# Batch 0 of an attention-and-MLP kernel: scores before transposes, a second load queue, an earlier normalise at the seam

## The chip, the cores and the metric

The kernel runs on one core of one Trainium2 chip. The metric is the device time of one execution in microseconds (us), as the median of several executions. "Span" is the part that the profile covers, about 1.8 us less than the time. Each run also lists the mean clock granted to TensorE (PE), where 1.000 means that no half-speed stretch is on record. The clock's record begins 4.6 to 7.1 us into the span, so the first warm-up matmuls, which start 0.43 us apart, twice the 0.216 us seen later at a granted clock of 1.00, are not in it.

## The reference

For 8 batches, 12 heads, 448 positions and a head size of 64, softmax attention with one added to the denominator; the result, as 3584 rows of 768, goes through a two-layer MLP with a squared ReLU.

```
scores = q @ k.T / 8
e      = exp(scores - max)
attn   = e / (sum(e) + exp(-max) + 1e-09)
x      = (attn @ v), heads side by side      # 3584 x 768
out    = (relu(x @ w_in) ** 2) @ w_out       # 768 -> 2048 -> 768
```

## The kernel before

Work goes by *units*. A unit is one pair of heads of one batch. Batch 0 is cut in two (192 and 256 query columns), so units 0 to 5 and 6 to 11 are batch 0, unit 12 is the first of batch 1, and so on. For one unit PE makes scores (two halves, `c` = 0 and 1), ACT takes exp, DVE adds the exps up (`es`), PE makes row sums and the product with v, ACT makes the reciprocal by Ln and Exp (`rcp`), and DVE multiplies (`normalise`, tile `xt`). When a block of `xt` is complete, MLP products are queued, and `drain` spreads them through the following units. Batches 0 and 1 are transposed on PE: DVE regroups q and k (`flatq`, `flatk`), PE transposes, DVE copies the result into `qk`.

```python
def load_natural(b, p0, p1):
    raw = b == 0 and p1 <= 2
    for n, r in (("q", q_r), ("k", k_r)):
        src = r[b, :, 2 * p0:2 * p1]
        if raw:                       # fp32, hardware queue of SP
            t = nat.tile([P, 2, RUN, D], FP32, name=f"{n}r{p0}")
            nc.sync.dma_start(out=t, in_=src)
        else:                         # cast to fp16 on the way, GpSimd's queue
            t = nat.tile([P, NPAIR, RUN, D], FP16, name=f"{n}n{p0 // 3}")
            nc.gpsimd.dma_start(out=t[:, 0:2 * (p1 - p0)], in_=src)
...
# the order of the loads; all but the first two go to GpSimd's one queue
load_natural(0, 0, 1); load_natural(0, 1, 2); load_natural(0, 2, 3); load_v(0, 0, 3)
load_natural(0, 3, 6); load_v(0, 3, 6)
for i in range(4): load_win(i, 8)
load_natural(1, 0, 3)
for i in range(4, 8): load_win(i, 8)
load_natural(1, 3, 6); load_v(1, 0, 3)
...
for i in range(NU + 1):               # the unit loop, shortened
        scores(u, et, 0)
        if i == 0: keep_warm(8)       # matmuls on zeros, for the clock
        if i in transpose_at: transposes(*transpose_at[i])
        if i in regroup_at: regroup(*regroup_at[i])
        if i < NPAIR: keep_warm(1)
        drain(share * 0.45)
        scores(u, et, 1)
    if prev:
        rcp = row_sums(prev, pes); values(prev, pet, xp, 0); values(prev, pet, xp, 1)
    ...                               # add_chunks(u) and drain, three steps
    if prev:
        normalise(prev, xp, rcp)
        if i - 1 in ready: ...        # queue MLP work, set share
```

The softmax here doesn't subtract the row's maximum and nothing guards it: scores larger than these inputs give would overflow.

## Time and profile before

| | before |
|---|---|
| time, median of the first 3 runs | 433.17 us (432.72 to 435.53) |
| span of the profiled run | 432.0 us |
| PE busy | 421.2 us, 97% |
| mean clock of the profiled run | 0.992 |
| last matmul to the end of the span | 4.06 us |

The kernel is in three parts: a head up to about 52 us, in which loads, ACT, DVE and PE take turns to be late; a middle, in which PE never stops; and a tail, in which the last rows leave. The views are shown and read in the prediction below.

### The profile page before, as it was taken

What the parts mean: (1) busy time and instruction counts of PE and PEld (TensorE: products, weight loads), DVE (VectorE), ACT (ScalarE), POOL (GpSimd) and SP (SyncE); (2) the same over time, 40 slices, a digit from 0 to 9 for tenths busy, and PEclk for the clock granted to TensorE, in tenths of its full rate; (3) what the DMA queues carried; (4) which work ended last, traced back from release to release, by engine and by line L of the source; (5) the groups of instructions that cost most, each with busy time, mean ns of one, the idle gap of its engine ahead of it and who ended that gap; (6) DMA issues with size and microseconds to landing.
All of it is one profiled execution on the core that took longest, in us unless ns stands there. A gap on an engine that the chain in (4) does not pass through costs nothing.

```text
span 432.0 us, 9194 instructions
## 1 busy us (share of the span) xinstructions
PE 421.2 (97%) x3979; PEld 248.6 (58%) x3979; DVE 244.6 (57%) x487; ACT 248.2 (57%) x361; POOL 33.5 (8%) x52
## 2 busy tenths in 40 slices
PE   8989899999999999999999999999999999999996
PEld 3556575554465666555456665655556566564463
DVE  3857595268822586348842488348762379338700
ACT  2989767764565756674456755764555665740011
POOL 8441100010000100010000100030000000000000
PEclk9989899999999999999999999999999999999999
DMA  9999999299312893259811697039902200020022
GB/s 175 197 197 203 209 220 199 75 154 200 69 38 76 145 212 66 73 83 216 125 38 56 102 212 130 38 67 206 189 0 74 75 2 2 38 73 2 0 74 73
DMA packets 78953, 47.33 MB, mean 110 GB/s; under 512 B 50624, under 2 KB 74944, under 8 KB 78528
## 3 DMA queue, kind: packets, MB, share of 16 engines
q0 software_dynamic: 24608, 22.40, 32.7%
q1 hardware_dynamic: 54304, 24.34, 25.3%
q8 instruction: 31, 0.51, 0.5%
q14 instruction: 10, 0.08, 0.1%
HBM read 45.71 MB, written 19.32 MB: 151 GB/s over the span
## 4 chain that ended last, share of the span: by engine, by line
PE 93%; ACT 3%; DVE 1%; DMA 1%; issue 1%; SPq 0%; ACTq 0%
PE mp L254 38%; PE mp L252 31%; PE sp L186 9%; PE xp L222 8%; PE mp L230 3%; PE sp L174 2%; ACT et L154 2%; DMA kr<-in_k_dram 1%; PE mp L146 1%; PE mp L372 1%; ACT lnz L233 1%; ACT rcp L234 0%; DVE es L203 0%; DVE es L207 0%; DVE qk L149 0%
## 5 line engine op out<-in xcount | busy, mean ns | idle before, releaser
L154 ACT ACTIVATE et<-sp 112x896 f16<-112x896 f32 (+2 forms) x192 | 166.2, 914 | 112.6 <-PE sp L186 92.0
L199 DVE TENSOR_TENSOR es<-et 112x896 f16<-112x896 f16 x84 | 51.5, 621 | 103.9 <-ACT et L154 103.8
L274 DVE TENSOR_SCALAR rt<-mp 128x512 f16<-128x512 f32 (+1 forms) x120 | 75.9, 632 | 35.9 <-PE mp L252 23.9
L254 PE MATMUL mp<-xt,win 128*128 128x512 f16 (+3 forms) x457 | 86.0, 341 | 1.5 <-DVE xt L242 1.5
L254 PE MATMUL mp<-wout,g 128*128 128x512 f16 (+1 forms) x471 | 82.3, 330 | 0.0
L252 PE MATMUL mp<-wout,g 128*64 128x256 f16 (+1 forms) x850 | 71.9, 322 | 0.0
L252 PE MATMUL mp<-xt,win 128*64 128x512 f16 (+3 forms) x814 | 71.3, 328 | 0.0
L254 PEld LDWEIGHTS <-win 128*128 128x128 f16 x457 | 42.2, 99 | 38.6 <-issue 3.7
L254 PEld LDWEIGHTS <-g 128*128 128x128 f16 x471 | 44.4, 98 | 33.9 <-issue 2.7
L292 ACT ACTIVATE ot<-mp 128x512 f32<-128x512 f32 (+1 forms) x56 | 27.3, 487 | 63.3 <-PE mp L254 51.6
L252 PEld LDWEIGHTS <-g 128*64 128x64 f16 x850 | 47.7, 110 | 19.5
L252 PEld LDWEIGHTS <-win 128*64 128x64 f16 x814 | 45.8, 112 | 22.2 <-issue 0.5
L276 DVE TENSOR_TENSOR g<-rt 128x512 f16<-128x512 f16 (+1 forms) x124 | 49.4, 399 | 6.6 <-ACT rt L272 2.4
L222 PE MATMUL xp<-et,vn 112*64 112x448 f16 (+2 forms) x432 | 46.1, 335 | 0.0
L186 PE MATMUL sp<-qk 64*112 64x224 f16 x576 | 42.8, 268 | 0.0
L186 PEld LDWEIGHTS <-qk 64*112 64x112 f16 x576 | 26.9, 127 | 25.4 <-issue 25.4
L233 ACT ACTIVATE lnz<-mp,one_b 128x448 f32<-128x448 f32 (+2 forms) x54 | 32.3, 598 | 1.8 <-PE mp L230 1.6
L242 DVE TENSOR_TENSOR xt<-xp,rcp 128x448 f16<-128x448 f32 (+2 forms) x54 | 30.5, 565 | 2.5 <-ACT rcp L234 2.5
L222 PEld LDWEIGHTS <-vn 112*64 112x64 f16 x432 | 24.6, 111 | 10.2 <-issue 0.4
L234 ACT ACTIVATE rcp<-lnz 128x448 f32<-128x448 f32 (+2 forms) x54 | 28.9, 535 | 1.7
L79 POOL DMA_DIRECT2D vn<-in_v_dram x10 | 8.9, 890 | 243.3 <-PE xp L222 230.5
L201 DVE TENSOR_TENSOR es<-es 112x896 f16<-112x896 f16 x42 | 26.1, 622 | 1.0
(36 smaller groups left out, 136.7 us busy)
## 6 DMA issues: line engine op xcount, KB each, us to landing
out_dram<-ot SPq DMA_DIRECT2D x12, 384.0 KB, 2.4
vn<-in_v_dram POOLq DMA_DIRECT2D x6, 672.0 KB, 9.1
stage_q<-in_q_dram POOLq DMA_DIRECT2D x5, 676.0 KB, 11.2
stage_k<-in_k_dram POOLq DMA_DIRECT2D x5, 676.0 KB, 14.2
win<-in_moe_w_in_dram POOLq DMA_DIRECT2D x8, 384.0 KB, 14.7
wout<-in_moe_w_out_dram POOLq DMA_DIRECT2D x4, 768.0 KB, 19.6
out_dram<-ot SPq DMA_DIRECT2D x8, 288.0 KB, 2.6
out_dram<-ot SPq DMA_DIRECT2D x8, 192.0 KB, 2.7
```

The costliest lines, as they stand in the source:

```text
L154: nc.scalar.activation(out=out_, in_=in_, func=AF.Exp, scale=scale)
L186: nc.tensor.matmul(sp[:, odd, h * (S // 2):(h + 1) * (S // 2)], qk[r, which, kx:kx + 2 * P - 1:2], qk[r, 0, x:x + S // 2], start=True, sto ...
L199: nc.vector.tensor_add(f[:, step], e[:, 2 * step], e[:, 2 * step + 1])
L222: nc.tensor.matmul(xp[64 * h:64 * h + 64, 0:n], vns[b][:, 2 * pr + h, kk, :], of_head(chunk(et, u, c, kk), u, h), start=(kk == 0), stop=(k ...
L233: nc.scalar.activation(out=lnz[:, 0:n], in_=zp[:, 0:n], func=AF.Ln, bias=one_b)
L234: nc.scalar.activation(out=rcp[:, 0:n], in_=lnz[:, 0:n], func=AF.Exp, scale=-1.0)
L242: nc.vector.tensor_mul(xts[b // 2][:, pr, c:c + n], xp[:, 0:n], rcp[:, 0:n])
L252: nc.tensor.matmul(out_[x:x + 64], lhsT[:, x:x + 64], rhs, start=start, stop=stop)
L254: nc.tensor.matmul(out_, lhsT, rhs, start=start, stop=stop)
L274: nc.vector.tensor_scalar(out=rt[:, 0:m], in0=hp[:, 0:m], scalar1=0.0, scalar2=None, op0=ALU.max)
L276: nc.vector.tensor_mul(g[:, 0:m], rt[:, 0:m], rt[:, 0:m])
L292: nc.scalar.activation(out=ot[:, n0:n1], in_=op[:, 0:n1 - n0], func=AF.Copy, scale=OUT_SCALE)
```

## The change

It tries to shorten the head: q and k of the first three pairs come over two hardware queues (q1 and q10), pair 3 comes before pairs 4 and 5, both score tiles of a unit precede the transposes for the next, four warm-ups fewer follow the first scores, normalise at the seam between units 5 and 6 moves up, two Relus move from ACT to DVE, and the last store is cut in two.

```diff
-        raw = b == 0 and p1 <= 2
+        raw = b == 0 and p1 <= 3
...
-                nc.sync.dma_start(out=t, in_=src)
+                (nc.sync if n == "q" else nc.scalar).dma_start(out=t, in_=src)
...
-    load_natural(0, 3, 6)
+    load_natural(0, 3, 4)
+    load_natural(0, 4, 6)
...
-        nc.scalar.activation(out=lnz[:, 0:n], in_=zp[:, 0:n], func=AF.Ln, bias=one_b)
-        nc.scalar.activation(out=rcp[:, 0:n], in_=lnz[:, 0:n], func=AF.Exp, scale=-1.0)
+        nc.scalar.activation(out=rcp[:, 0:n], in_=zp[:, 0:n], func=AF.Ln, bias=one_b)
+        nc.scalar.activation(out=rcp[:, 0:n], in_=rcp[:, 0:n], func=AF.Exp, scale=-1.0)
...
-            if t0 == 0:
+            if t0 == 0 and f0 % 8 == 0:
                 nc.scalar.activation(... func=AF.Relu)
...
+                if n1 == DM or t0 + ts * 128 + 128 == NT:
+                    store(t0 + ts * 128, ot, 0 if n1 < DM or t0 + ts * 128 + 128 < NT else n0, n1)
...
             if i == 0:
-                keep_warm(8)
+                keep_warm(4)
+            elif i < NPAIR:
+                keep_warm(1)
+                scores(u, et, 1)
+            if i == NPAIR:
+                rcp = row_sums(prev, pes)
+                values(prev, pet, xp, 0)
+                values(prev, pet, xp, 1)
+                normalise(prev, xp, rcp)
+                take_up(i - 1)
             if i in transpose_at:
                 transposes(*transpose_at[i])
-            if i in regroup_at:
+            if i in regroup_at and i < NPAIR:
                 regroup(*regroup_at[i])
-            if i < NPAIR:
-                keep_warm(1)
-            drain(share * 0.45)
-            scores(u, et, 1)
+            drain(share[0] * (0.45 if i != NPAIR else 0.0))
+            if i == 0 or i >= NPAIR:
+                scores(u, et, 1)
...
+        if i in regroup_at and i >= NPAIR:
+            regroup(*regroup_at[i])
```

More of the change, by code (lines that the diff above doesn't have):

```diff
@@ L60 @@
     ctx.enter_context(tc.manual_schedule())
-    nc.scalar.preload_act_table_set("natural_log_exp_and_others")
     win = persist.tile([128, DCH, DF], FP16, name="win")
@@ L71 @@
     wout_r = moe_w_out.rearrange("(c p) f -> p c f", p=128)
-    vns, qks, xts, naturals, flats, stages = {}, {}, {}, {}, {}, {}
+    whole, vns, qks, xts, naturals, flats, stages = {}, {}, {}, {}, {}, {}, {}
     def load_v(b, p0, p1):
@@ L87, in load_natural @@
                 t = nat.tile([P, 2, RUN, D], FP32, name=f"{n}r{p0}")
-                nc.sync.dma_start(out=t, in_=src)
+                (nc.sync if n == "q" else nc.scalar).dma_start(out=t, in_=src)
             else:
-                t = nat.tile([P, NPAIR, RUN, D], FP16, name=f"{n}n{p0 // 3}")
-                nc.gpsimd.dma_start(out=t[:, 0:2 * (p1 - p0)], in_=src)
+                if p0 % 3 == 0:
+                    whole[n] = nat.tile([P, NPAIR, RUN, D], FP16, name=f"{n}n{p0 // 3}")
+                t = whole[n][:, 2 * (p0 % 3):2 * (p0 % 3 + p1 - p0)]
+                nc.gpsimd.dma_start(out=t, in_=src)
             for pr in range(p0, p1):
@@ L230, in row_sums @@
             nc.tensor.matmul(zp[64 * h:64 * h + 64, 0:n], ones, of_head(total, u, h), start=True, stop=True)
-        lnz = z_pool.tile([128, S], FP32, name="lnz")
         rcp = z_pool.tile([128, S], FP32, name="rcp")
-        nc.scalar.activation(out=lnz[:, 0:n], in_=zp[:, 0:n], func=AF.Ln, bias=one_b)
-        nc.scalar.activation(out=rcp[:, 0:n], in_=lnz[:, 0:n], func=AF.Exp, scale=-1.0)
+        nc.scalar.activation(out=rcp[:, 0:n], in_=zp[:, 0:n], func=AF.Ln, bias=one_b)
+        nc.scalar.activation(out=rcp[:, 0:n], in_=rcp[:, 0:n], func=AF.Exp, scale=-1.0)
         return rcp
@@ L279, in mlp_in, with store @@
             yield n / 2.4
+    def store(c, ot, n0, n1):
+        end = c + 128
+        while c < end:
+            b = c // S
+            step = RUN if b in ON_PE else 2
+            rows = out[b * S:(b + 1) * S, n0:n1].rearrange("(p t) m -> t p m", t=step)
+            t, p = c % S // (S // step), c % (S // step)
+            m = min(S // step - p, end - c)
+            o = c + 128 - end
+            nc.sync.dma_start(out=rows[t, p:p + m, :], in_=ot[o:o + m, n0:n1])
+            c += m
     def mlp_out(t0, n):
@@ L292, in mlp_out @@
                 nc.scalar.activation(out=ot[:, n0:n1], in_=op[:, 0:n1 - n0], func=AF.Copy, scale=OUT_SCALE)
+                if n1 == DM or t0 + ts * 128 + 128 == NT:
+                    store(t0 + ts * 128, ot, 0 if n1 < DM or t0 + ts * 128 + 128 < NT else n0, n1)
                 if n1 < DM:
                     yield (n1 - n0) / 2.4
-            c = t0 + ts * 128
-            end = c + 128
-            while c < end:
-                b = c // S
-                step = RUN if b in ON_PE else 2
-                rows = out[b * S:(b + 1) * S, :].rearrange("(p t) m -> t p m", t=step)
-                t, p = c % S // (S // step), c % (S // step)
-                m = min(S // step - p, end - c)
-                o = c + 128 - end
-                nc.sync.dma_start(out=rows[t, p:p + m, :], in_=ot[o:o + m, :])
-                c += m
             yield (DM - 512) / 2.4
@@ L314 @@
     nc.vector.memset(one_b, 1.0 / GS)
-    load_natural(0, 0, 1)
-    load_natural(0, 1, 2)
-    load_natural(0, 2, 3)
+    for pr in range(3):
+        load_natural(0, pr, pr + 1)
+    nc.scalar.preload_act_table_set("natural_log_exp_and_others")
     load_v(0, 0, 3)
@@ L379, with take_up @@
     et = es = None
-    share = 0.0
+    share = [0.0]
+    def take_up(i):
+        if i in ready:
+            for part in ready[i]:
+                queue(*part)
+            share[0] = left[0] / NPAIR
     for i in range(NU + 1):
@@ L396 @@
             if i == 0:
-                keep_warm(8)
+                keep_warm(4)
[8 more added lines that the diff above has]
+                take_up(i - 1)
             if i in transpose_at:
                 transposes(*transpose_at[i])
-            if i in regroup_at:
+            if i in regroup_at and i < NPAIR:
                 regroup(*regroup_at[i])
-            if i < NPAIR:
-                keep_warm(1)
-            drain(share * 0.45)
-            scores(u, et, 1)
-        if prev:
+            drain(share[0] * (0.45 if i != NPAIR else 0.0))
+            if i == 0 or i >= NPAIR:
+                scores(u, et, 1)
+        if prev and i != NPAIR:
             rcp = row_sums(prev, pes)
@@ L411 @@
                 keep_warm(1)
+        if i in regroup_at and i >= NPAIR:
+            regroup(*regroup_at[i])
         halved[0] = u is not None
-        drain(share * 0.15)
+        drain(share[0] * 0.15)
         for step in range(3):
@@ L416 @@
                 add_chunks(u, et, es, step)
-            drain(share * (0.15, 0.1, 0.15)[step])
+            drain(share[0] * (0.15, 0.1, 0.15)[step])
         halved[0] = False
-        if prev:
+        if prev and i != NPAIR:
             normalise(prev, xp, rcp)
-            if i - 1 in ready:
-                for part in ready[i - 1]:
-                    queue(*part)
-                share = left[0] / NPAIR
+            take_up(i - 1)
         if u and b and pr == 2 and b + 1 < B:
```

## The prediction

> **What bounds the kernel now.** I read the page first, then busy times by stage, then the chain of waits over the first 60 us, then the stalls and landings of that stretch. The engine row:
>
> ```profile
> PE 421.2 (97%) x3979; PEld 248.6 (58%) x3979; DVE 244.6 (57%) x487; ACT 248.2 (57%) x361; POOL 33.5 (8%) x52
> ```
>
> PE is busy 97% of 432.0 us, so the room is small, and the busy times of five stretches say where it lies (start:end and length, then busy us with instruction counts, granted clock, DMA share, GB/s):
>
> ```profile
> 0.00:7.66 7.66, 5.82 (x25) 2.34 (x26) 2.45 (x8) 1.28 (x1) 6.49 (x14) 1.00 0.83 176
> 7.66:22.91 15.25, 14.64 (x161) 8.21 (x161) 11.21 (x30) 12.51 (x23) 7.97 (x10) 1.00 1.43 192
> 22.91:43.31 20.40, 17.57 (x287) 13.25 (x287) 13.75 (x35) 17.68 (x29) 5.30 (x7) 0.92 1.39 200
> 43.31:51.95 8.64, 7.21 (x59) 4.77 (x57) 5.73 (x14) 6.20 (x10) 1.98 (x3) 0.80 1.16 211
> 51.95:428.40 376.45, 375.98 (x3453) 220.04 (x3451) 211.42 (x404) 210.57 (x302) 11.74 (x19) 1.00 0.49 98
> 428.40:432.04 3.64, 0.00 (x0) 0.00 (x0) 0.00 (x0) 0.00 (x0) 0.00 (x0) 1.00 0.28 108
> ```
>
> From 51.95 to 428.40 PE is idle 0.47 us in all. The change takes nothing out of that stretch, so whatever is won before 51.95 moves the end one for one, and the only other place is the 3.64 us tail. Before 51.95, ACT is the busiest engine of the middle stages (12.51 of 15.25, 17.68 of 20.40), and the DMA share is over 1.3 from 7.66 on (transfers overlap in an engine): the loads never pause there.
>
> The same table cut at steps of 3.413 us back and forth from the clock's first drop:
>
> ```profile
> 23.20:26.61 3.41, 1.89 (x24) 1.19 (x25) 1.84 (x5) 3.13 (x5) 1.54 (x2) 1.00 1.45 197
> 26.61:30.02 3.41, 3.41 (x40) 2.42 (x40) 1.75 (x4) 1.81 (x3) 1.51 (x2) 0.50 1.46 201
> 36.85:40.26 3.41, 2.38 (x44) 1.68 (x43) 3.21 (x8) 3.17 (x5) 0.00 (x0) 1.00 1.36 205
> 43.68:47.09 3.41, 2.06 (x20) 1.12 (x18) 2.32 (x7) 3.41 (x6) 0.15 (x1) 1.00 1.16 212
> 47.09:50.50 3.41, 3.33 (x20) 2.39 (x20) 2.13 (x4) 2.42 (x5) 1.83 (x3) 0.50 1.16 209
> ```
>
> Two windows with PE busy 55% and 60% are each followed by 3.41 us at half clock; one with 70% is not. The second drop falls on PE-bound work and costs up to 1.7 us.
>
> The waits of PE and DVE in the first 60 us (total, times, longest) and the start of the chain name the stalls that the change aims at:
>
> ```profile
> 1.19 4.46 DMA kr<-in_k_dram
> ```
>
> ```profile
> PE mp L230 <- DVE es L207: 1.7, 3, 1.0
> PE mp L254 <- DVE xt L242: 1.5, 1, 1.5
> DVE g L276 <- ACT rt L272: 2.4, 3, 1.7
> ```
>
> The first k lands at 5.65; at the seam (24.8 to 26.25) the first MLP product waits for the normalised block; and the squares wait behind ACT's Relu, which holds back the es additions queued behind them on DVE and then the row sums on PE (38.29).
>
> Last, a thing the change does not touch: k of pairs 3 to 5 of batch 1. It is issued at 24.11 and takes 14.9 us, so it lands at 39.01, and DVE copies it at once:
>
> ```profile
> L91 POOL DMA_DIRECT2D kn<-in_k_dram x1: 769/769/769, 24.1 to 24.1; - x1
> ...
> DMA to landing us min/median/max: 14.9/14.9/14.9
> ```
>
> ```profile
> 39.21 0.29 DVE L139 COPY flatk<-kn 112x512 f16<-112x512 f16 x1
> 39.42 0.68 DVE L203 TENSOR_TENSOR es<-et 112x1024 f16<-112x1024 f16 x1
> ```
>
> Only 0.2 us separate landing and use,[...] the es addition of unit 10 comes right behind that copy.
>
> [...]
>
> **The change part by part.**
>
> *Head.* q on SP and k on ACT: kr is issued at about 0.75 instead of 1.19[...]. Both of pair 0 should land near 4.2 (qr alone took 2.5 us[...]), against 5.65. ACT pays three issues of about 0.45 and then the table load, done near 3.5, long before its first exp. But nine warm-up matmuls, at half clock 0.43 us each, hold PE until about 5.05, so the transposes move from 6.16 to about 5.1 only. Then: transposes 0.7 (cold), copy 0.64, three warm-ups and four scores: first exp at about 7.0, was 7.66. Warm-ups fall from 8 to 4 in unit 0 (0.215 us each, 0.86), and both score tiles of a unit precede the transposes of the next, so ACT's gaps of 1.94, 0.38 and 0.18 us shrink. Walking PE, DVE and ACT in their new order with the durations above, the end of rcp of unit 0 moves from 13.51 to about 12.0, provided pair 2 lands by 9. From there ACT is nearly full: 1.62 for two exps plus 0.78 for Ln and Exp per unit, the old pace of 9.4 us for four units. DVE, busy 4.75 of 5 us between 15 and 20, is no faster. Gain at the seam: about 1.3 to 1.5 us.
>
> *Seam.* Normalise of unit 5 comes ahead of exp (6, second half); its Ln starts behind one exp instead of two (about 1.0 us sooner), and MLP products start in unit 6 instead of 7. Of PE's 1.5 us wait about 0.7 stays, and that window's clock drop probably goes. exp of unit 8 would come near 27.6, was 30.14: 2.5 us gained.
>
> *Relu.* Two of four Relus go from ACT (0.58 each) to DVE (0.69 each), which ends the waits of squares on ACT. Over units 8 to 11 that is another 0.5 to 1 us. Up to here the paper gain is 3 to 3.7 us.
>
> *What gives it back.* The kernel would now want k of batch 1, pair 3, at about 35.5, and it lands near 39. The stream before it is saturated (about 195 GB/s of fp16 written), and the change removes no byte read: pair 2 only moves to a hardware queue. I estimate 38.7, 0.6 sooner to 0.1 later than 39.0. DVE stands at that copy, unit 10's es behind it, and PE stands at the transposes. So es of unit 10 starts near 39.0, was 39.42, and most of the 3 us lead is lost there. What survives: exp and Relu work that ACT has done during the wait. After it come transposes 0.5, eight products 0.45, scores 0.4: exp (11, second half) at 40.4 (was 41.56), Ln and Exp 0.9, exps of unit 12 at 42.3 (was 43.31), without the 0.6 us Relu in their midst: PE-bound work begins 1.25 us sooner than before.
>
> *Clock.* The wait of 1.5 to 2 us for k probably makes a window under 60% busy, so one drop near 39 to 44 (slowing the 1.35 us of PE work above: up to 1.3 lost). Unit 12 stays thin on PE (about 2.7 us of work in 4.4 us of ACT), so a second drop into PE-bound work is still likely, unless the first overlaps unit 12 (1.7 won). These about balance.
>
> *Tail.* The last store is cut into 512 and 256 columns; the final piece is 128 KB instead of 384. Landings here hardly depend on size (384 KB 2.4 us, 192 KB 2.7, 96 KB 2.2), so 0.2 us. *In-place rcp*: Ln now waits for the previous normalise; in every unit that I looked at the normalise is done first. Zero.
>
> Sum: 1.25 + 0.2 = 1.45 if the landing binds, with the clock neutral. That is 431.7.
>
> **Rivals.**
> 1. *The landing does not bind* (hardware queues use slack in the first 8 us, the stream arrives 2 us sooner). For it: early traffic was 175 GB/s in the first slice, under the 200 later. Against: no slice of the next five is under 197. Then 3.5 + 0.2, about 429.4; with one clock drop fewer, 427.7.
> 2. *The clock decides.* Fewer warm-ups and longer waits give a drop at the head too[...]. About 433.5.
> 3. *The head's loads get worse*: three streams at once delay pair 2 or pairs 4 and 5 (13.43 before, wanted at about 13.9). DVE would block there; but any loss is hidden by the 39 us gate. About 432.
>
> **Range and chances.** Weights of 0.75, 0.2 and 0.05 on the main line, rival 1 and the rest give about 431.3. Medians of before spread by up to 2.8 us in three runs. Range 428.6 to 433.6. Two per cent is 8.7 us; all gains together with no clock drop reach 5.6. So: faster 0.03, within 0.96, slower 0.01.
>
> **What would show it.** Right: a DVE wait for k of batch 1 of 1.5 us or more ending near 39, es of unit 10 within 0.5 us of 39.2, first exp near 7.0, no clock drop just after the seam, Relu waits gone. Wrong: the copy of that k starting before 37 without a wait, which means that the stream moved and the gain is 3 us or more; or PE idle after 52.

## The result, and the profile after

The changed kernel takes 430.63 us (median of 6 runs, 430.11 to 432.50), the kernel before 433.48 us (6 runs). The ratio is 0.9939, with a 95% interval of 0.9909 to 0.9968. Ratios are the mean time of one kernel's fast runs over that of the other's of the same rounds, so not quite the ratio of the medians. That is 0.6% faster, inside 2%.

The first profile of the changed kernel fell in the slowest of its six runs (432.50 us, mean clock 0.988). Its engine row, and its busy times by stage with the columns of the table in the prediction:

```profile
PE 421.4 (98%) x3975; PEld 248.1 (58%) x3975; DVE 246.6 (57%) x489; ACT 247.6 (57%) x359; POOL 33.2 (8%) x52
```

```profile
7.66:22.91 15.25, 13.99 (x138) 7.72 (x137) 10.80 (x27) 10.84 (x19) 7.73 (x10) 0.78 1.45 197
22.91:43.31 20.40, 18.02 (x307) 13.19 (x302) 15.02 (x37) 18.16 (x29) 5.30 (x7) 1.00 1.39 201
51.95:427.00 375.05, 375.01 (x3447) 219.59 (x3444) 211.47 (x403) 209.46 (x301) 11.67 (x19) 1.00 0.49 98
427.00:430.70 3.70, 0.43 (x4) 0.13 (x2) 0.00 (x0) 0.38 (x1) 0.00 (x0) 1.00 0.30 106
```

The middle is as before: PE idle 0.04 us in 375. But in the first stage ACT did less than before (10.84 us against 12.51), at a granted clock of 0.78. In this run the head became slower. Two windows of the same table show where:

```profile
8.15:11.57 3.42, 2.16 (x30) 1.32 (x27) 2.49 (x6) 2.32 (x4) 1.67 (x4) 1.00 1.45 196
11.57:14.98 3.41, 3.41 (x27) 1.62 (x24) 1.99 (x7) 2.38 (x4) 2.33 (x3) 0.50 1.45 197
```

The clock was halved for two windows, 11.57 to 18.39, and again from 45.70 to 49.11. A quieter run was needed to see the change itself; it is the first experiment. Even so, the waits of PE and DVE in the first 60 us answer to those shown of before:

```profile
DVE g L276 <- ACT rt L272: 2.3, 2, 2.1
PE mp L231 <- DVE es L208: 2.2, 3, 1.0
PE mp L252 <- DVE xt L242: 0.2, 1, 0.2
```

The seam's wait for the normalised block fell from 1.5 to 0.2 us. The other two did not fall in this run: the first remaining Relu still held a square for 2.1 us. Nor did DVE wait for k of batch 1, pair 3: it landed near 39.1, and DVE came to it at 39.60 only, the lead having been lost to the clock.

The tail shrank more than the whole head did in this run. From the last matmul (427.44) to the end it took 3.27 us, against 4.06. The last store's landing, before and after:

```profile
DMA to landing us min/median/max: 2.3/2.3/2.3
```

```profile
DMA to landing us min/median/max: 1.7/1.7/1.7
```

### The profile page after: what moved, and what is told of

It is laid out like the page before. It is cut to its first block, busy times and chain, and to the rows that moved or that the text cites.

```text
span 430.7 us, 9136 instructions
## 1 busy us (share of the span) xinstructions
PE 421.4 (98%) x3975; PEld 248.1 (58%) x3975; DVE 246.6 (57%) x489; ACT 247.6 (57%) x359; POOL 33.2 (8%) x52
## 4 chain that ended last, share of the span: by engine, by line
PE 92%; DVE 2%; ACT 2%; DMA 2%; issue 1%; ACTq 0%
PE mp L254 37%; PE mp L252 31%; PE sp L187 9%; PE xp L223 8%; PE mp L231 3%; PE sp L175 2%; DMA kr<-in_k_dram 2%; ACT et L155 1%; PE mp L147 1%; PE mp L376 1%; DVE es L204 1%; DVE qk L150 0%; ACT rcp L233 0%; DVE xt L242 0%; DVE es L208 0%
## 5 line engine op out<-in xcount | busy, mean ns | idle before, releaser
L274 DVE TENSOR_SCALAR rt<-mp 128x512 f16<-128x512 f32 (+1 forms) x122 | 77.4, 635 | 35.3 <-PE mp L252 24.1
L254 PE MATMUL mp<-xt,win 128*128 128x512 f16 (+3 forms) x456 | 84.8, 339 | 0.0
L252 PE MATMUL mp<-xt,win 128*64 128x384 f16 (+3 forms) x816 | 71.2, 325 | 0.2 <-DVE xt L242 0.2
L233 ACT ACTIVATE rcp<-mp,one_b 128x448 f32<-128x448 f32 (+2 forms) x54 | 32.2, 597 | 3.1 <-PE mp L231 2.8
L234 ACT ACTIVATE rcp<-rcp 128x448 f32<-128x448 f32 (+2 forms) x54 | 28.9, 535 | 1.7
```

Of the source, the lines that this page charges most:

```text
L233: nc.scalar.activation(out=rcp[:, 0:n], in_=zp[:, 0:n], func=AF.Ln, bias=one_b)
L234: nc.scalar.activation(out=rcp[:, 0:n], in_=rcp[:, 0:n], func=AF.Exp, scale=-1.0)
L252: nc.tensor.matmul(out_[x:x + 64], lhsT[:, x:x + 64], rhs, start=start, stop=stop)
L254: nc.tensor.matmul(out_, lhsT, rhs, start=start, stop=stop)
L274: nc.vector.tensor_scalar(out=rt[:, 0:m], in0=hp[:, 0:m], scalar1=0.0, scalar2=None, op0=ALU.max)
```

## The experiments

Every timed run was listed with its mean clock. One window of 3.41 us at half speed takes 0.004 off that mean (the profiled run of before, with two, has 0.992), so runs can be sorted by the number of clock drops. Kernel before, 33 runs in three sets of rounds (the six of the result have no clock on record); changed kernel, 12 runs (six at first, six in the first experiment):

| mean clock | before, us (runs) | changed, us (runs) |
|---|---|---|
| 1.000 | 432.27 (5) | 430.32 (6) |
| 0.997 to 0.999 | 432.49 (5) | 430.30 (1) |
| 0.994 to 0.996 | 432.93 (9) | 431.18 (4) |
| 0.990 to 0.993 | 434.33 (13) | none |
| 0.988 | 436.04 (1) | 432.50 (1) |
| all, mean | 433.41 (33) | 430.79 (12) |

At clock 1.000 the change is worth 432.27 - 430.32 = 1.95 us. The means over all runs differ by 2.62. The other 0.67 us goes, by this sorting, to the clock, which the changed kernel loses less often. The experiments are compared at equal clock where they can be; all use five rounds, six runs each. They ran on three chips (e1 to e4, e5 to e8, e9 to e11), on which the kernel before took 432.09, 432.34 and 432.47 us at clock 1.000 (2, 2 and 1 runs). So differences of 0.4 us between sets are not told from the chip; the ratio to before is free of that, as before ran in the same rounds.

| run | edit on the changed kernel | median us | ratio to before | mean at clock 1.000 (runs) | runs at 0.999 or more |
|---|---|---|---|---|---|
| e1_again | none | 430.44 | 0.9938 | 430.34 (3) | 4 |
| e2_split | pair 3 of batch 1 loaded alone | 430.28 | 0.9923 | 428.27 (1) | 1 |
| e3_kw8 | eight warm-ups in unit 0 | 430.26 | 0.9933 | 430.18 (4) | 5 |
| e4_tail_whole | last store whole | 431.14 | 0.9956 | 431.10 (4) | 4 |
| e5_loads_old | loads of batch 0 as before | 431.33 | 0.9970 | 430.90 (4) | 4 |
| e6_order_old | order of units 0 to 5 as before | 430.42 | 0.9933 | 430.28 (5) | 6 |
| e7_relu_act | Relus on ACT as before | 431.59 | 0.9968 | none | 0 |
| e8_seam_old | seam as before | 432.10 | 0.9973 | 431.48 (2) | 2 |
| e9_before_split | e2's edit on the kernel *before* | 433.14 | 0.9996 | 432.10 (1) | 1 |
| e10_split_warm | e2's edit, warm-ups in unit 12 | 428.68 | 0.9888 | 428.63 (5) | 6 |
| e11_split_warm_head | e10's, two warm-ups in unit 1 | 429.27 | 0.9905 | 429.41 (4) | 6 |

### e1_again: the same kernel, a quieter run

> The changed kernel once more[...]. Its first profile fell in the slowest of its six runs: three windows of 3.41 us at half clock (11.57 to 18.39 and 45.70 to 49.11), while three other runs had a mean clock of 1.000. Theory (the landing of k of batch 1, pair 3, near 39 us takes back the head's lead when the clock does not): with no drop at the head, the end of rcp of unit 0 near 11.9, the lead over the kernel before at exp of unit 8 about 2 us or more, then a DVE wait for that k of at least 1 us ending near 39, and a time of 430.1 to 430.9. Rival (the landing does not bind, the first profile's clock drop is all that ate the lead): no such wait in a profile without an early drop, and the copy of that k before 38.

Its profiled run has clock 1.000 and a span of 428.7 us. DVE and ACT in order of time, the bracket giving the engine's idle time just before and what ended it:

```profile
36.61 0.29 DVE L140 COPY flatq<-qn 112x512 f16<-112x512 f16 x1
39.12 0.29 DVE L140 COPY flatk<-kn 112x512 f16<-112x512 f16 x1 [2.21 <-DMA kn<-in_k_dram]
39.33 0.68 DVE L204 TENSOR_TENSOR es<-et 112x1024 f16<-112x1024 f16 x1
```

```profile
40.68 1.02 ACT L155 ACTIVATE et<-sp 112x1024 f16<-112x1024 f32 x1 [1.84 <-PE sp L175]
...
42.43 3.32 ACT L155 ACTIVATE et<-sp 112x896 f16<-112x896 f32 x4
```

DVE stands 2.21 us at the copy of k of batch 1, pair 3; the es addition of unit 10 starts at 39.33, where the kernel before had it at 39.42. Everything that the head won by then is gone, except what ACT did while it waited. By stage:

```profile
7.66:22.91 15.25, 14.09 (x173) 8.20 (x172) 11.64 (x31) 13.66 (x26) 7.83 (x10) 1.00 1.45 197
22.91:43.31 20.40, 16.69 (x286) 12.48 (x281) 15.22 (x36) 16.46 (x25) 5.30 (x7) 1.00 1.39 201
```

ACT is ahead after the first stage (13.66 us done, before 12.51) and stands idle in the second (16.46 of 20.40, before 17.68). So the lead existed: the exp of unit 8 came at 27.41, against 30.14 before, 2.7 us ahead. By the exps of unit 12 it was 0.9 us (42.43 above, against 43.31). This run, then the kernel before:

```profile
27.41 1.99 ACT L155 ACTIVATE et<-sp 112x1024 f16<-112x1024 f32 x2
```

```profile
30.14 1.02 ACT L154 ACTIVATE et<-sp 112x1024 f16<-112x1024 f32 x1 [1.15 <-PE sp L174]
...
43.31 1.71 ACT L154 ACTIVATE et<-sp 112x896 f16<-112x896 f32 x2
```

A second wait of the kind goes untested: DVE stood 1.41 us for k of pairs 0 to 2 of batch 1, until 26.80 (0.67 us, until 27.06, in the kernel before). No experiment moves that load, so what it costs is not known.

### e2_split: that load sooner

```diff
-    load_natural(1, 3, 6)
+    load_natural(1, 3, 4)
+    load_natural(1, 4, 6)
```

> q and k of batch 1, pair 3, are loaded alone, ahead of pairs 4 and 5, as the change did in batch 0. They should land near 36.5 to 37 instead of 39. Theory (the landing binds in runs without an early clock drop): 1 to 2 us faster than the changed kernel, about 429. Rival (it does not bind): the same within 0.4 us.

The copy no longer waits:

```profile
36.87 0.28 DVE L140 COPY flatq<-qn 112x512 f16<-112x512 f16 x1
37.07 0.29 DVE L140 COPY flatk<-kn 112x512 f16<-112x512 f16 x1
```

At clock 1.000 the one run took 428.27 us, 2.05 less than the changed kernel's 430.32. The median hardly moved (430.28), because five of the six runs lost the clock right afterwards. The windows of the profiled run:

```profile
41.24:44.66 3.42, 2.06 (x23) 1.13 (x20) 3.02 (x9) 3.42 (x6) 0.00 (x0) 1.00 1.17 213
44.66:48.07 3.41, 3.41 (x21) 2.36 (x21) 2.04 (x4) 2.29 (x4) 1.98 (x3) 0.50 1.15 207
```

Unit 12 has no MLP work to fill PE, so ACT bounds it, and then the half clock falls on the PE-bound part. The wait was exchanged for a clock drop. Of the two theories, the landing binds (one run at clock 1.000; e10 repeats it); but the expectation of a median near 429 failed.

### e3_kw8: more warm-ups at the head

```diff
-                keep_warm(4)
+                keep_warm(8)
```

> Eight warm-up matmuls in unit 0 again instead of four (0.86 us more PE work at full clock). If the clock drop at the head is what costs time in the slower runs of the changed kernel: no drop before 20 us in any profile, mean clock at most one window short (0.996 or more), and a narrower spread. If the landing of k hides what happens before 39 us: median within 0.5 us of the changed kernel. If the head's length decides: 0.9 us slower.

At clock 1.000: 430.18 us, the same as the changed kernel's 430.32. Four more warm-ups of 0.216 us in the head cost nothing, as the landing hides them. One run of six still lost the clock, and the profiled one did so at 45.5, not at the head. Whether they protect the head can't be told from six runs.

### e4_tail_whole: the last store in one piece

```diff
-                if n1 == DM or t0 + ts * 128 + 128 == NT:
-                    store(t0 + ts * 128, ot, 0 if n1 < DM or t0 + ts * 128 + 128 < NT else n0, n1)
+                if n1 == DM:
+                    store(t0 + ts * 128, ot, 0, n1)
```

> The last 128 rows are stored in one piece again, after their second half. The prediction gave the tail 0.2 us; the traces read 4.06 us from the last matmul to the end before and 3.27 after, so 0.79. By the traces: 0.6 to 0.9 us slower than the changed kernel, and 4.0 to 4.1 us from the last matmul to the end. By the prediction: 0.2 us slower.

431.10 us against 430.32 at clock 1.000: the cut store is worth 0.78 us. The trace agrees: the landing takes 2.4 us again, and 3.98 us pass from the last matmul (425.86) to the end of the span (429.84).

### e5_loads_old: the loads of batch 0 as before

```diff
-        raw = b == 0 and p1 <= 3
+        raw = b == 0 and p1 <= 2
...
-                (nc.sync if n == "q" else nc.scalar).dma_start(out=t, in_=src)
+                nc.sync.dma_start(out=t, in_=src)
...
-    load_natural(0, 3, 4)
-    load_natural(0, 4, 6)
+    load_natural(0, 3, 6)
```

(with the table load of ACT, 1.28 us in the trace of the kernel before, back at the start, and the tiles of pair 2 as before)

> All of the changed kernel but the loads of batch 0: q and k of pairs 0 and 1 by SP alone, pair 2 by GpSimd, pairs 3 to 5 together. The first k should land near 5.6 again (4.5 in the changed kernel) and the end of rcp of unit 0 come 0.7 to 1.5 us later than 11.9. Theory (the landing of k of batch 1, pair 3, near 39 hides what the head wins; in the last profile of the changed kernel DVE waited 2.21 us for it): at equal clock (1.000) the same within 0.4 us as the changed kernel, 430.3, with a shorter wait for that k. Rival (the head's loads are worth what they move the first exp): 0.7 to 1.5 us slower.

At clock 1.000: 430.90, so 0.58 us slower; the medians differ by 0.7 to 0.9. The four runs at that clock spread from 430.02 to 431.36, so the size is not sure; of the other two, one took 435.43 us at a mean clock of 0.980. My expectation of the first k was wrong: DVE could copy it at 4.35 in this run, while the profile of the kernel before shows 5.68, with the same two queues. What the old loads cost came later, where pairs 3 to 5 are one transfer:

```profile
13.61 0.29 DVE L142 COPY flatk<-kn 112x512 f16<-112x512 f16 x1 [1.25 <-DMA kn<-in_k_dram]
```

The end of rcp of unit 4 was at 23.31, against 21.28 in e1: 2.0 us lost at the seam. At the copy of k of batch 1, DVE had nothing left to wait for (38.85), and the exps of unit 12 began at 42.75 against 42.43. So of 2.0 us about 0.3 us reached unit 12 in the trace, and about 0.6 us the time. The landing hides most of it; whether all is not settled, between the theory's 0.4 and the rival's 0.7.

### e6_order_old: the order of units 0 to 5 as before

```diff
-                keep_warm(4)
-            elif i < NPAIR:
-                keep_warm(1)
-                scores(u, et, 1)
+                keep_warm(8)
...
+            if i < NPAIR:
+                keep_warm(1)
             drain(share[0] * (0.45 if i != NPAIR else 0.0))
-            if i == 0 or i >= NPAIR:
-                scores(u, et, 1)
+            scores(u, et, 1)
```

> All of the changed kernel but the order in units 0 to 5: second score tile after the transposes, eight warm-ups in unit 0. Theory (hidden by the landing): at equal clock within 0.5 us of 430.3, the DVE wait for k shorter by what the head loses. Rival (the order is worth its 1 to 1.5 us of ACT gaps): 431.3 or more at clock 1.000.

430.28 us at clock 1.000: no difference. In the trace the end of rcp of unit 0 is 13.70 against 11.86, so 1.84 us were lost there, 1.08 of them still at unit 4; and the wait for k is shorter:

```profile
38.41 0.29 DVE L140 COPY flatk<-kn 112x512 f16<-112x512 f16 x1 [0.70 <-DMA kn<-in_k_dram]
```

Half of that shorter wait is a sooner landing (38.41 against 39.12), and the exps of unit 12 begin sooner by as much (41.72 against 42.43), although the head was 1.84 us later: the stage after follows the landing, not the head. Both score tiles together are worth nothing here as long as the landing binds.

### e7_relu_act: the Relus on ACT as before

```diff
-            if t0 == 0 and f0 % 8 == 0:
+            if t0 == 0:
```

> All of the changed kernel but the Relus: all four of the first block on ACT again. The second of the moved ones falls into unit 12, after the landing, between exps that bound that stage. Theory: 0.3 to 0.7 us slower at equal clock (0.6 us of ACT in unit 12; the other is before the landing and hidden). Rival (all Relus off the path): the same within 0.2 us. Second rival (both count): 1.0 us or more slower.

No run kept a clock of 1.000. At 0.994 to 0.996 it took 431.35 us (5 runs), the changed kernel 431.18 (4 runs): the same within 0.2. In the trace the exps of unit 12 start at 42.67, 0.24 later than in e1, not 0.6. But over all six runs its mean is 431.65 against 430.79: the Relus' place is worth 0.9 us, by this sorting nearly all by way of the clock (six runs against twelve, on another chip). I had not expected that.

### e8_seam_old: the seam as before

```diff
-            if i == NPAIR:
-                rcp = row_sums(prev, pes)
-                values(prev, pet, xp, 0)
-                values(prev, pet, xp, 1)
-                normalise(prev, xp, rcp)
-                take_up(i - 1)
...
-            drain(share[0] * (0.45 if i != NPAIR else 0.0))
+            drain(share[0] * 0.45)
```

(with normalise and the regroups at their old places)

> All of the changed kernel but the seam: normalise of unit 5 at its old place, first MLP products in unit 7, regroups of batch 1 at their old place. Theory: most of what it loses (1 to 2.5 us at exp of unit 8) is inside the wait for k, so 0 to 0.8 us slower at equal clock; but the 1.5 us PE wait at the seam comes back, and with it a clock drop near 27 in most runs, so fewer runs at clock 1.000. Rival (the seam is worth its 1.5 us wait): 1.5 us or more slower at equal clock.

The wait at the seam is back, with the clock drop behind it (25.52 to 28.94; the granted clock of 20 to 40 us is 0.91, in e1 1.00):

```profile
PE mp L254 <- DVE xt L242: 1.7, 2, 1.5
```

At clock 1.000 it took 431.48 us (two runs), 1.16 slower, more than the 0.8 that I allowed. The trace of the profiled run doesn't explain that: its last matmul ends at 425.71, only 0.30 later than in e1 (425.41), although the clock dropped on the way; and its last store landed in 2.7 us instead of 1.7. One late landing accounts for most of the 1.3 us by which its span is longer. Whether the two runs at clock 1.000 had the same is not known. What the seam is worth is left open between 0.3 and 1.2 us; the chip of this set may be 0.25 us of it.

### e9_before_split: the same load sooner in the kernel before

The diff is that of e2, on the kernel before (with both transfers into one tile).

> The kernel before, with q and k of batch 1, pair 3, loaded alone as in e2_split, and nothing else. Theory (the landing binds only a kernel that arrives early; before missed it by 0.2 us): the same as the kernel before within 0.4 us at equal clock. Rival (that load is a bottleneck in its own right): 1 us or more faster than before.

433.14 us, ratio 0.9996. By clock: 432.10 (one run) against 432.27, and 433.09 (three at 0.994 to 0.996) against 432.93. In the trace DVE comes to that k when it did before, and does not wait for it (in e2, with the same edit, it copied it at 37.07 without a wait):

```profile
39.36 0.29 DVE L142 COPY flatk<-kn 112x512 f16<-112x512 f16 x1
```

The load was no bottleneck before; it became one because the change got there early.

### What goes before a clock drop

PE's busy share tells most drops, but not all: in the first 70 us of the profiles 12 windows were at most 65% busy, and 11 of them were followed by a drop. The twelfth, 59% busy (36.9 to 40.3 in e1), was not, while windows 63% and 65% busy (8.15 and 42.29 in the first profile after) were. Another quantity separates them all. In the trace of the kernel before, between 52 and 427 us, matmuls of 512 columns on the whole array that follow each other start every 0.216 us, and those of 256 columns every 0.109 us (medians). So 256 columns more take 0.107 us, which is 2.4 columns a ns. Each half-clock stretch in the clock's record of that trace lasts 3.413 us; the two start at 26.61 and 47.09, six such lengths apart. For each window of 3.413 us at full clock I added up, from the matmul records, active rows x active columns x moving columns, over what a full 128 x 128 array could stream in the window at 2.4 columns a ns.

```
13 profiles of this case          windows   filled share
followed by half clock                 11   0.280 to 0.354
not followed                         1570   0.369 and more
```

Only windows that end before the last matmul are counted. The first ten profiles (9 and 1207 windows; the expectation below says nine) gave the two bounds; the last three came afterwards and kept to them, e9 with its two drops. A recount from the traces gave the same bounds, and found that columns alone, rows x columns, or the filled share without the transposes leave windows on the wrong side. Still, the gap is narrow, it is that of one family of kernels, and against the busy share it rests on the one window of e1. By this measure 64-row scores and 112-column transposes fill less than they look busy (before, 43.68 to 47.09: PE 60% busy, filled share 0.29), while a warm-up on the whole array adds its 512 columns in full.

### e10_split_warm: the load sooner, and warm-ups where PE waits for ACT

```diff
 (e2's diff, and)
+            if i == 2 * NPAIR:
+                keep_warm(3)
             if i == 0 or i >= NPAIR:
                 scores(u, et, 1)
...
+            if i == 2 * NPAIR:
+                keep_warm(2)
```

> The changed kernel with pair 3 of batch 1 alone, and five warm-up matmuls in unit 12 (three ahead of its second scores, where PE waits for ACT, two after values of unit 11). In nine profiles every clock drop followed a window of 3.41 us whose matmuls filled 0.354 or less of what a full array streams, and none of 1207 windows at 0.369 or more was followed by one; five warm-ups add 0.31 to a window. Theory: no drop after 41 us, and nearly all runs at clock 1.000 with 428.0 to 428.8 us, as the one such run of e2_split (428.27). Rival (the warm-ups delay the scores of unit 12, or the drop has another cause): 429.5 or more.

All six runs are at 0.999 or more, with a median of 428.68 us (428.14 to 429.07); the ratio to the kernel before is 0.9888 (0.9863 to 0.9913). It beats both kernels; two of the six (428.93 and 429.07) lie above the expected 428.8. The run doesn't tell the filled share from the busy share, as warm-ups raise both. Unit 12 in the trace:

```profile
40.00:44.00 4.00, 3.45 (x31) 1.68 (x28) 3.80 (x9) 3.97 (x7) 0.00 (x0) 1.00 1.17 212
```

```profile
40.87 3.32 ACT L155 ACTIVATE et<-sp 112x896 f16<-112x896 f32 x4
```

ACT is full (3.97 of 4.00), so the warm-ups delay nothing that counts there, and the exps of unit 12 begin at 40.87 against 42.43 in e1.

### e11_split_warm_head: two more warm-ups in unit 1

```diff
 (e10's diff, and)
                 scores(u, et, 1)
+                if i == 1:
+                    keep_warm(2)
```

> As e10_split_warm, and two more warm-ups in unit 1, ahead of the transposes that wait for k of pair 2, where the first profile of the changed kernel lost the clock. Theory: as e10 within 0.3 us in its median, and its slowest run no more than 1 us above its median (no early drop). Rival (0.43 us of PE work at the head shows now that the landing is out of the way): 0.3 to 0.5 us slower than e10.

429.27 us, and 429.41 against 428.63 at clock 1.000: 0.78 us slower, more than the 0.43 us of PE work added. With the landing out of the way, a change at the head shows again. The two traces differ by 0.21 us only (exps of unit 12 at 41.08 against 40.87, last matmul at 424.10 against 423.89), so where the rest went is not known. The clock at the head was not lost in either set, so the warm-ups protected nothing that was seen.

## Why the prediction was right or wrong

The mechanism was right (431.3 us predicted, 430.63 measured), and the sum of its main line was low, 1.45 us against 2.62. One step failed, the clock, and one was mis-sized, the tail. By its steps:

- **What bounds.** Right. PE was idle 0.04 us between 51.95 and 427 after. Three readings were loose. Of the 0.47 us of idle PE, 0.42 us lie after the last matmul (427.98), so the tail was 4.06 us and not 3.64. From 7.66 to 22.91 PE was busier than ACT (14.64 us against 12.51), though 6.04 us of that were warm-ups. And the DMA share was 1.16, not over 1.3, after 43.31.
- **Head.** Right, to 0.2 us, in the quiet run: first exp at 7.17 (predicted 7.0), end of rcp of unit 0 at 11.86 (12.0). That pair 0 lands near 4.2 was near enough (DVE copies q at 4.45 and k at 4.98); the figure was my estimate, from the 2.5 us of one load of q. No run isolates the second queue; e5 undoes it together with other loads.
- **Seam.** Right: exp of unit 8 at 27.41 (27.6), and no clock drop behind the seam in the profiles that keep the new seam; with the old one it came back (e8).
- **What gives it back.** Right, and shown rather than argued, where the clock holds: the wait of 2.21 us ending at 39.12 (1.5 or more, near 39), es at 39.33 (within 0.5 of 39.2), exp (11, second half) at 40.68 (40.4), exps of unit 12 at 42.43 (42.3). At clock 1.000 the parts ahead of the tail give 1.95 - 0.78 = 1.17 us, where the prediction had 1.25. e2 and e9 make the cause plain: the same load moved is worth about 2 us in the changed kernel (2.05 in e2's one run at clock 1.000, 1.69 in e10's five, with warm-ups) and nothing in the one before. e6 shows the other side: 1.84 us of the head undone cost nothing.
- **Relu.** Its direct gain was off: "another 0.5 to 1 us" is, at equal clock, within 0.2 us, because the landing hides the first one and the second delays unit 12 by 0.24 us. Its waits shrank rather than vanished (2.4 us before, 0.6 in e1).
- **Clock.** The step that failed. It held that the wait for k makes "a window under 60% busy" and so costs a drop, and that drops balance. In e1 the wait was 2.21 us, its window 59% busy, and no drop followed, while windows 63% and 65% busy were followed by one; what separates all windows is the filled share (0.354 or less against 0.369 or more). And the drops did not balance: 7 of 12 runs of the changed kernel had a mean clock of 0.999 or more, 5 of 33 before, which by the sorting above is 0.67 of the 2.62 us.
- **Tail.** Mis-sized: "Landings here hardly depend on size ... so 0.2 us" measured 0.78 (e4). I had compared medians over the whole execution, and the smaller stores in them are issued in pairs. The last store moves its data alone: 384 KB landed in 2.3 us, 128 KB in 1.7. That is 0.6 of it. The other 0.2 passes between the landing and the end of the span (1.30 us before, 1.12 after); why is not known.
- **In-place rcp.** No experiment isolates it. In e1 no wait of Ln for a normalise is listed among ACT's waits.
- **Rivals.** The first (the landing does not bind) fell by e1 and e2. The second (the clock decides) describes single runs, such as the first profile, not the median. The third fell: no late pair 4 or 5 after; it is the old loads that wait for them (e5).

Of the 1.2 us by which the sum was too low, tail and clock are each about 0.6; the head had its size. These two errors did not cancel. That the time still came close is partly luck: 0.4 us of the forecast of 431.3 were weight given to a rival that fell.

## What to carry to other kernels

Before working on a head, find the next thing whose arrival hardly moves (here a load of 336 KB in a full queue, 14.9 us from issue to landing, which landed between 38.4 and 39.1 in every profile that left it in its place) and ask how early the kernel may reach it; time won beyond that is lost until the load moves too. When experiments differ by less than a half-clock window is worth, sort the runs by mean clock first. Where PE waits on another engine for some us, try matmuls over the whole array in the waiting time: with five of them in unit 12 all six runs had a mean clock of 0.999 or more (e10), without them one of six (e2).
